# Strassen's scheme for one batch's gate and value products, fewer filler matmuls and operand copies on GpSimd in an attention and gated-layer kernel

## The chip, the cores and the metric

One core of one Trainium2 chip runs the whole program; seven other cores are idle. The metric is the device time of one execution in microseconds (us). Three executions of the kernel before took 910.0, 910.58 and 910.41 us, median 910.41. Engines are called as in the profile: PE (TensorE matmuls), PEld (its weight loads), DVE (VectorE), ACT (ScalarE), POOL (GpSimd), SP (SyncE, which here only issues DMAs).

## The reference

Attention with a pooled query feeds a gated layer; all in float32, with weights that come as 64-bit numbers. The tolerance is that of float32, so the kernel computes most products in split precision (below).

```python
# B, H, S, D = 4, 8, 1152, 64
q_pool = q.reshape(B, H, S // 2, 2, D).mean(axis=3)            # 576 queries a head
scores = np.matmul(q_pool, k.transpose(0, 1, 3, 2)) / np.sqrt(D)
scores = scores - np.max(scores, axis=-1, keepdims=True)
attn = np.exp(scores)
attn = attn / (np.sum(attn, axis=-1, keepdims=True) + 1e-09)
attn_out = np.matmul(attn, v)
x = attn_out.transpose(0, 2, 1, 3).reshape(2304, 512)          # 4 batches of 576 rows
gate = 1.0 / (1.0 + np.exp(-(x @ w_gate)))                     # 512 -> 1536
val = x @ w_val                                                # 512 -> 1536
out = (gate * val) @ w_out                                     # 1536 -> 512
```

## The kernel before

**Split precision.** A float32 operand is stored as two fp32r tiles: a rounded copy `hi` (made by ACT) and the rest `lo` (made by POOL or DVE). A product is three matmuls: hi times hi, hi times lo, lo times hi. Nearly all matmuls stream 288 columns, half of a batch's 576 rows.

**Attention.** 32 heads go in 16 pairs, four pairs to a batch. For each head `head_operands` (L470; `first_head`, L380, for head 0) loads q and k (slots `qr`, `kr`, one each), makes the split operands `QA`/`QB`, `KA`/`KB`, computes the score maxima on PE and DVE (`maxima`, L537, reduction at L550; L452 and L457 for head 0), and writes minus the maximum as a diagonal block into `QB` (`diags`, L371), so that the second score matmul subtracts it. The last 64 queries of both heads of a pair are maximised together from a shared copy `KP`/`QP`, which two DMAs per head (L577, L578) copy from `KA` and `QA`/`QB`. `half` (L624) then does 9 key chunks for each half of the queries: scores (L650), exp (ACT, L654 and L683), its rest (DVE, L686), and the products with v (L693, L697; L668 for the heads of batch 0, `WHOLE`). POOL sums the denominators (L715 to L725), and L770 adds them on PE. `normalise` (L778) divides and splits the result into the `x` tiles.

**Gated layer.** `gated` (L866) runs once a batch: twelve blocks of 128 hidden features in three thirds of four. In each third come four blocks of gate and value (`product`, L877: 4 chunks of the input features by 3 matmuls, 12 matmuls of 288 columns for each block, kind and half: gate to tanh at L929, value times gate at L935, hi at L939, lo at L943) and then four output blocks (`wo`, 12 matmuls for each block and half, added up by L969 and L971). `convert` (L817) turns the 64-bit weights into split float32 during batch 0 and stores them in HBM (`wg_d`, `wo_d`); `weights` (L893) loads them back for each batch. The last batch's wo weights use the three `K` slots, which attention has left by then.

**Warm-up.** `busy` (L989) issues filler matmuls of 192 columns whose result nobody reads, four to a step; `BUSY` (L354) is the number of steps, 18.

**Order.** Each engine runs its instructions in program order, and that order is a table: `Plan.op` lists every step with its engine, and `placed` (L216) puts the steps into the order of `ORDER` and gives each tile the slot that `PLACES` names. The durations, due times and priorities in the calls of `pl.op` are what a planner elsewhere made the tables from; at run time they have no effect. `PSUM` has eight banks (slots `b`).

Of the kernel before, what the change touches and what calls it, by code (L numbers as in the profile page):

```python
# [29 lines left out]
    "YdOSE<z4WC+sJL^UUFNxo$_|h1Dm+T+!oFUOSo-ZB7ng!?hm(*`_1j(zHxiF{agTca(lVI90Ak$yWAHp6*$1{=Du==xn0~3?jU!R`^g>Q4spl0"  # L30
    "@7!$uGB<}m#U1BPb7#1J+zIX+mxiCgr{X#OB$rxD&7bAc^5?lEz~$%iA#d^?AMh8rS^PYH7f*P~TYNe`Gk=Mj$*1S@@fSIp&%*0`0zN;Vhd21F"
    "{7ybEpOBBoXXmr=4xft$d}849G5kF~1CRNPd=5S*pPSz$$LA?X3K%HJCj&+JLVN)}0)_eHARZ{n@8Q#cM0^Us_)MTQA0JfU6Z0kcGJM1r<5Pnx"
    "Tmn#$FU6+?2|*IR5?_KZ36t_=`Qm&Pz8pWFFV9!z7w`x8WPCc11tjNd^4GaSU^!o%uf^BqtMZHal%N`4hhM?h;B$c`{C@rr--ut$rw0xA!~7b4"
    "A-|H}%h%;IfQI}kJ|j5DH|7`dnL!i2IiD3Y<y-P=`F(snzBRv&Z^bv`TkzRH8@@hYUdY5><!*2t_zFThz9Zj>&ki>7TluB@CcZO&pKr^z=W~FY"
# [197 lines left out]
def attention_glu_kernel(ctx: ExitStack, tc: tile.TileContext, qT, kT, vt_in, v, wg, wv, wo, out):  # L232
# [114 lines left out]
    def pool(n, two=True):  # L347
        return 0.18 + 2.35e-3 * n if two else 0.2 + 0.9e-3 * n

    def dma(kb):  # L350
        return 0.15 + kb / 285

    AHEAD = 50
    BUSY = 18  # L354
    KEEP = 0.15
    LAST_GATE = 215
    QLP = lambda u: 1 <= u < 2 * H

    WHOLE = lambda u: u < H
    KLD = lambda u: u >= 16  # L360
# [717 lines left out]
```

## Time and profile before

| | |
|---|---|
| runs | 910.0, 910.58, 910.41 us |
| the profiled execution | 910.93 us |
| its span, first to last instruction | 909.1 us |
| PE busy | 899.6 us (99%), 6371 matmul records |
| DVE, ACT, POOL busy | 651.6, 650.8, 666.7 us |
| moved by DMA | 166.27 MB, 183 GB/s on average |

The profiled execution took 1.8 us more than its span; that is what lies around the instructions. Matmuls are pipelined and the profile models their ends, so two neighbours overlap in "busy"; what one costs is a stretch's time divided by the matmuls that started in it.

### The profile page before, as it was taken

The numbers are of one execution on the slowest core, as the hardware profiler recorded it, in microseconds if no ns is written. First come the engines' busy times: TensorE is split into PE (matmuls) and PEld (weight loads), VectorE is DVE, ScalarE is ACT, GpSimd is POOL, SyncE is SP. The second block draws the span as 40 slices with busy tenths as digits, with TensorE's granted clock in tenths as the row PEclk, the third lists the DMA queues.
The fourth block names the chain that finished last, engine by engine and source line by source line (L and its number), as shares of the span: only waits on it lengthen the run. The fifth ranks groups of instructions, "written<-read, shape, count | busy, mean of one in ns | idle before, by whom it ended". The sixth has DMA issues, their size and how long they took to land.

```text
span 909.1 us, 18593 instructions
## 1 busy us (share of the span) xinstructions
PE 899.6 (99%) x6371; PEld 879.5 (97%) x6371; DVE 651.6 (72%) x1427; ACT 650.8 (72%) x1703; POOL 666.7 (73%) x669
## 2 busy tenths in 40 slices
PE   8999999999999999999999999999999999999998
PEld 7888888999999999999999999999999999999998
DVE  6777788988998998878787887878778774410122
ACT  4878899999998887777777787677787657421211
POOL 6646466989999889988888999888898778521111
PEclk9999999999999999999999999999999999999999
DMA  6898999778887585545563544672734423444532
GB/s 166 226 290 228 279 285 245 241 237 286 294 242 242 175 263 170 158 140 152 154 172 129 137 110 149 209 208 87 195 101 142 152 86 117 143 152 152 186 139 76
DMA packets 57615, 166.27 MB, mean 183 GB/s; under 512 B 17392, under 2 KB 21744, under 8 KB 51376
## 3 DMA queue, kind: packets, MB, share of 16 engines
q1 hardware_dynamic: 57360, 164.78, 60.0%
q8 instruction: 50, 0.82, 0.4%
q14 instruction: 45, 0.37, 0.1%
q10 hardware_dynamic: 160, 0.30, 0.1%
HBM read 132.12 MB, written 23.59 MB: 171 GB/s over the span
## 4 chain that ended last, share of the span: by engine, by line
PE 94%; DVE 3%; DMA 2%; ACT 1%; issue 1%; ACTq 0%; DVEq 0%
PE bank L886 49%; PE bank L650 16%; PE bank L544 8%; PE bank L668 6%; PE bank L693 6%; PE bank L697 6%; PE bank L770 1%; PE bank L991 1%; DMA wg_d<-cs 1%; DMA cr<-in_wv_dram 1%; DVE pm L457 1%; DVE pm L550 1%; ACT e L654 0%; DVE KB L521 0%; DVE el L686 0%
## 5 line engine op out<-in xcount | busy, mean ns | idle before, releaser
L886 PE MATMUL bank<-x,wg 128*128 128x288 f32 x2304 | 371.5, 295 | 0.0
L886 PEld LDWEIGHTS bank<-x,wg 128*128 128x128 f32 x2304 | 331.4, 188 | 0.4
L654 ACT ACTIVATE eh<-bank 128x288 fp32r<-128x288 f32 x432 | 170.9, 411 | 84.0 <-PE bank L650 60.4
L550 DVE TENSOR_REDUCE pm<-bank 128x1 f32<-128x384 f32 x375 | 197.8, 549 | 45.1 <-PE bank L544 41.9
L686 DVE TENSOR_TENSOR el<-bank,eh 128x288 fp32r<-128x288 f32 x432 | 187.5, 451 | 56.1 <-ACT bank L683 26.7
L650 PE MATMUL bank<-QA,KA 128*128 128x288 f32 x576 | 171.0, 303 | 0.4 <-DVE pm L550 0.4
L683 ACT ACTIVATE bank<-bank 128x288 f32<-128x288 f32 x432 | 170.7, 409 | 0.2
L650 PE MATMUL bank<-QB,KB 128*128 128x288 f32 x576 | 166.2, 295 | 1.2 <-DVE QB L375 1.2
L715 POOL TENSOR_TENSOR acc<-acc,eh 128x576 f32<-128x576 f32 x92 | 134.3, 1460 | 18.3 <-ACT eh L654 14.5
L943 POOL TENSOR_TENSOR g<-sg,g 128x288 fp32r<-128x288 f32 x96 | 78.4, 822 | 88.9 <-ACT g L939 86.9
L886 PE MATMUL bank<-g,wo 128*128 128x288 f32 x864 | 143.3, 295 | 0.0
L886 PEld LDWEIGHTS bank<-g,wo 128*128 128x128 f32 x864 | 125.8, 188 | 0.1
L544 PE MATMUL bank<-KA,QA 128*128 128x384 f32 x375 | 121.8, 350 | 0.4 <-DVE pp L550 0.4
L697 PE MATMUL bank<-el,vt 128*128 128x288 f32 x432 | 119.6, 295 | 0.0
L650 PEld LDWEIGHTS bank<-QA,KA 128*128 128x128 f32 x576 | 108.2, 188 | 3.4 <-ACT e L654 0.8
L650 PEld LDWEIGHTS bank<-QB,KB 128*128 128x128 f32 x576 | 108.2, 188 | 2.5 <-issue 1.4
L693 PE MATMUL bank<-eh,vt 128*128 128x288 f32 x432 | 108.5, 295 | 0.0
L935 DVE SCALAR_TENSOR_TENSOR sg<-sg,bank 128x288 f32<-128x288 f32 x96 | 43.0, 449 | 77.5 <-PE bank L886 57.1
L668 PE MATMUL bank<-e,ve 128*128 128x288 f32 x288 | 78.4, 407 | 1.6 <-ACT e L654 1.5
L697 PEld LDWEIGHTS bank<-el,vt 128*128 128x128 f32 x432 | 78.9, 188 | 0.3 <-DVE el L686 0.2
L521 POOL TENSOR_TENSOR KB<-kr,KA 64x576 fp32r<-64x576 f32 x46 | 65.7, 1435 | 17.4 <-ACT KA L515 12.5
L715 POOL TENSOR_TENSOR acc<-eh,eh 128x576 f32<-128x576 f32 x48 | 68.7, 1431 | 10.7 <-ACT eh L654 9.1
(86 smaller groups left out, 1378.1 us busy)
## 6 DMA issues: line engine op xcount, KB each, us to landing
wg<-wg_d SPq DMA_DIRECT2D x48, 1024.0 KB, 5.5
wo<-wo_d SPq DMA_DIRECT2D x36, 512.0 KB, 3.9
kr<-in_kT_dram SPq DMA_DIRECT2D x62, 288.0 KB, 4.9
wg_d<-cs SPq DMA_DIRECT2D x24, 512.0 KB, 5.4
qr<-in_qT_dram SPq DMA_DIRECT2D x31, 288.0 KB, 4.3
KP<-KA SPq DMA_DIRECT2D x30, 288.0 KB, 5.8
vr<-in_v_dram SPq DMA_DIRECT2D x24, 288.0 KB, 4.4
cr<-in_wg_dram SPq DMA_DIRECT2D x12, 512.0 KB, 5.7
```

Source lines behind the costliest of these rows:

```text
L544: nc.tensor.matmul(out=tl(m)[LO if t == 4 else ALL, 0:384], lhsT=lhs(t), rhs=rhs()[:, j * 384:(j + 1) * 384], start=True, stop=True)
L550: nc.vector.tensor_reduce(out=o, in_=tl(m)[p, 0:384], axis=AXX, op=ALU.max)
L650: nc.tensor.matmul(out=tl(m)[:, 0:GN], lhsT=tl(hd["k"])[k][:, ks], rhs=tl(hd["q"])[k][:, a:b], start=(k == 0), stop=(k == 1))
L654: nc.scalar.activation(out=ev(), in_=tl(m)[:, 0:GN], func=ACTF.Exp, scale=1.0 / 16.0)
L668: nc.tensor.matmul(out=tl(av[0])[:, 0:GN], lhsT=pair(c, 0), rhs=tl(h), start=(c == 0), stop=(c == NC - 1))
L683: nc.scalar.activation(out=p, in_=p, func=ACTF.Exp, scale=1.0 / 16.0)
L686: nc.vector.tensor_tensor(out=tl(el), in0=tl(m)[:, 0:GN], in1=ev().bitcast(F32), op=ALU.subtract)
L693: nc.tensor.matmul(out=tl(av[0])[:, 0:GN], lhsT=pair(c, w), rhs=ev(), start=(c == 0), stop=(c == NC - 1))
L697: nc.tensor.matmul(out=tl(av[1])[:, 0:GN], lhsT=pair(c, 1 - w), rhs=tl(el), start=(c == 0), stop=(c == NC - 1 and not mine_c))
L715: nc.gpsimd.tensor_tensor(out=tl(acc), in0=tl(old).bitcast(F32), in1=tl(eh).bitcast(F32), op=ALU.add)
L886: nc.tensor.matmul(out=ps[:, 0:GN], lhsT=l, rhs=r, start=(n == 0 and j == 0), stop=(n == 3 and j == 2))
L943: nc.gpsimd.tensor_tensor(out=g[:, 1, a:b], in0=tl(sg), in1=g[:, 0, a:b].bitcast(F32), op=ALU.subtract)
```

## The change

- The gate and value products of the last batch use Strassen's scheme in Winograd's form: two feature blocks by two halves of the 512 input features by two halves of the rows are seven products of half the depth (2 chunks by 3 matmuls) in place of eight. `gated` calls `two_rows` six times for the last batch, and that calls `seven` once for gate and once for value.
- For this `differences` makes four combinations of the `x` tiles once (T1 to T4: 11 DVE and 4 ACT steps for pair 14, and as many for pair 15), and `combinations` makes four combinations of the weights for each `seven` (S1 to S4: on DVE two additions of 512 columns and four of 256, then two `hi` on ACT and two `lo` of 512 columns on POOL). Products are added up by DVE from the banks.
- The output weights of the last batch lie in the two `wo` slots, no longer in the three `K` slots, which now hold mixed weights (`K`), and each fourth block of gate and value weights lies in `vt0` and `vt1`.
- `BUSY` is 6 in place of 18: 24 filler matmuls in place of 72.
- The `KP`/`QP` copies of pairs 1 to 3 are made by POOL, three copies for each head, in place of DMAs; the other pairs keep the DMAs.
- `FOLD` and `POOLSC` are always false here (u and due are never negative), so their branches do nothing.
- Both tables are new: 7375 steps in place of 7153.

Unpacked, the new `ORDER` says this. **PE** starts with five filler steps (20 matmuls), then the first third of the maxima of query tiles 2, 0 and 1 of head 0, then the sixth filler step, and no filler after it; before, fourteen steps (56) stood ahead of the first maximum and four more among the maxima. **SP** issues v of head 0 (L402) after q and k of head 1; before, it stood ahead of them. **From the last attention matmul (L770) to the last mixing of weights** the table has 528 matmuls on PE; on DVE 19 additions of 512 columns, 40 of 256 and 7 of 288 with both inputs in SBUF, 83 steps of 288 columns with one input in PSUM and one `norm`; on POOL 18 `lo` of 512 columns and 18 steps of 288; on ACT 75 steps. After that 285 matmuls, 46 steps of 288 columns on DVE and 2 and 8 on POOL follow. The last output block weights are loaded when the slot two blocks back is free.

```diff
-    BUSY = 18
+    BUSY = 6
+    KPP = lambda p: p < 4
...
+            if KPP(p):
+                def copy(k, h=h, r=r, w=w):
+                    o, i = (tl(kp)[0][r, SQ * k:SQ * k + SQ], tl(h["k"])[0][r, SQ * k:SQ * k + SQ]) if k < 2 else (
+                        tl(kp)[1][r, 64 * w:64 * w + 64], tl(h["q"])[w][r, 512:SQ])
+                    nc.gpsimd.tensor_copy(out=o, in_=i)
+                for k in range(3):
+                    got.append(pl.op("POOL", 0.7 if k < 2 else 0.2, lambda k=k, copy=copy: copy(k), need - 10 + w, ...
...
+    def differences(p, j, me, nm, s):
...
+            o = pl.op("ACT", act(GN), hi, at, after=after, uses=uses + ([h] if j else []), take=[] if j else [h])
+            x_done["T" + n, j] = pl.op("DVE", dve(GN), lo, at, after=[o], uses=uses + [h])
...
+        o = mix(t1, lambda: b1(0, 1), lambda: b1(0, 0), ALU.subtract, ...
+        o = mix(t1, t1, lambda: b1(1, 1), ALU.add, [old, fh], [o], s - 2)
+        o = mix(t1, t1, lambda: b1(1, 0), ALU.subtract, [old, fh], [o], s - 2)
+        s1 = split("1", t1, [fh], [o], s)
+        t2 = mix(t1, b22, t1, ALU.subtract, [me, fh], [nm, s1], s)
+        split("2", t1, [fh], [t2], s + 0.1)
+        o = mix(b22, b22, lambda: b1(0, 1), ALU.subtract, [me, old], [t2, x_done[p, 1]], s + 0.1)
+        t3 = mix(b22, b22, lambda: b1(1, 1), ALU.subtract, [me, old], [o], s + 0.1)
+        t4 = mix(b21, b21, t1, ALU.subtract, [me, fh], [t2, x_done[p, 0]], s + 0.2)
+        split("3", b22, [me], [t3], s + 0.2)
+        split("4", b21, [me], [t4], s + 0.3)
...
         def weights(kind, m_, at):
-            tag = "K" if kind == "wo" and ch == B - 1 else kind
-            wh = pl.hold(tag)
+            wh = pl.hold(kind)
...
+        def plain(m_, at):
+            whs = [pl.hold("vt0"), pl.hold("vt1")] if m_ % 4 == 3 else [pl.hold("wg")]
...
+        def combinations(i, s):
...
+            fh, sh = pl.hold("kr"), pl.hold("K")
...
+            def full(w, h):
+                nc.vector.tensor_tensor(out=f(h, A), in0=w(0, s, A).bitcast(F32), in1=w(1, s, A).bitcast(F32), op=ALU.add)
...
+            r0 = pl.op("DVE", dve(512), lambda: full(a0, f0), at - 7, after=[l0], uses=w0, take=[fh])
+            r1 = pl.op("DVE", dve(512), lambda: full(a1, f1), at - 7, after=[l1], uses=w1 + [fh])
+            s1 = mix((f1, R), (f1, L), (f1, R), ALU.add, [r1])
+            s3 = mix((f1, L), (f0, L), (f1, L), ALU.subtract, [r0, s1])
+            s2 = mix((f0, L), (f1, R), (f0, L), ALU.subtract, [s1, s3])
+            s4 = mix((f0, R), (f0, R), (f0, L), ALU.subtract, [s2])
...
+                o = pl.op("ACT", act(512), hi, at - 6, after=after, uses=[fh] + ([sh] if k else []), take=[] if k else [sh])
+                done.append(pl.op("POOL", pool(512), lo, at - 6, after=[o], uses=[fh, sh]))
...
+        def seven(i, s, put):
+            sw = combinations(i, s)
...
+                    def mm(j=j, x=x):
+                        for c, (h, l) in enumerate(((0, 0), (0, 1), (1, 0))):
+                            nc.tensor.matmul(out=tl(bank)[:, 0:GN], lhsT=w(h, j), rhs=x(l), ...
...
+            b, p, at = mult("A11", "11")
+            k1 = keep(s1, b, [p], at)
+            b, p, at = mult("S2", "T2")
+            k2 = plus(s2, b, s1, [p, k1], at)
+            b, p, at = mult("A12", "21")
+            put(0, 0, b, s1, [p, k1], at)
+            b, p, at = mult("S1", "T1")
+            k4 = plus(s4, b, s2, [p, k2], at)
+            b, p, at = mult("S3", "T3")
+            u2 = plus(s2, b, s2, [p, k2, k4], at)
+            put(1, 1, b, s4, [p, k4, u2], at)
+            b, p, at = mult("S4", "22")
+            put(0, 1, b, s4, [p, k4], at)
+            b, p, at = mult("A22", "T4")
+            put(1, 0, b, s2, [p, u2], at)
...
+                    nc.vector.tensor_tensor(out=ps, in0=ps, in1=tl(sh), op=ALU.add)
...
+            seven(i, 0, put_gate)
+            seven(i, 1, put_val)
...
+            if ch == B - 1:
+                two_rows(2 * third, gs)
+                two_rows(2 * third + 1, gs)
```

(`keep` is an ACT copy of a bank, `plus` a DVE addition of a bank and a kept tile; `put_gate` adds and takes tanh, `put_val` adds, multiplies by the gate, and splits as L935 to L943 did.)

## Rows read from the trace of the kernel before

**Rows 1.** The page: busy time of engines; the chain that ended last.
```profile
PE 899.6 (99%) x6371; PEld 879.5 (97%) x6371; DVE 651.6 (72%) x1427; ACT 650.8 (72%) x1703; POOL 666.7 (73%) x669
...
PE 94%; DVE 3%; DMA 2%; ACT 1%; issue 1%; ACTq 0%; DVEq 0%
```

**Rows 2.** Stretches: length, busy of PE, PEld, DVE, ACT, POOL (instructions), clock, DMA.
```profile
30.00:60.00 30.00, 30.00 (x164) 26.41 (x162) 23.14 (x48) 26.66 (x64) 16.60 (x16) 1.00 0.98 257
...
150.00:780.00 630.00, 629.25 (x4640) 627.47 (x4639) 514.70 (x1135) 503.86 (x1352) 550.70 (x545) 1.00 0.58 176
...
18.00:790.57 772.57, 770.22 (x5416) 751.26 (x5417) 621.66 (x1353) 622.63 (x1637) 634.90 (x625) 1.00 0.64 190
790.57:906.00 115.43, 115.39 (x870) 115.15 (x869) 20.36 (x48) 22.69 (x57) 20.66 (x26) 1.00 0.39 137
```

**Rows 3.** Busy time by stretch of the filler line L991: length, PE busy (matmuls started).
```profile
2.70:7.90 5.20, 5.17 (x24) 5.17 (x25) 1.00 1.08 249
8.30:11.50 3.20, 3.20 (x31) 3.20 (x30) 1.00 0.87 192
```

**Rows 4.** Timeline of the start: start, length, engine, line, operation.
```profile
6.14 0.55 DVE L418 TENSOR_TENSOR QA<-qr,QA 64x384 fp32r<-64x384 f32 x1
...
11.57 0.71 PE L452 MATMUL bank<-KA,QA 128*128 128x384 f32 x3
...
11.96 4.76 DVE L457 TENSOR_REDUCE pm<-bank 128x1 f32<-128x384 f32 x10 [5.27 <-PE bank L452]
17.89 0.37 PE L650 MATMUL bank<-QB,KB 128*128 128x288 f32 x1 [1.17 <-DVE QB L375]
...
19.85 1.87 PE L668 MATMUL bank<-e,ve 128*128 128x288 f32 x6
```

**Rows 5.** SP's issues at the start; landing of the first v loads (tile ve).
```profile
4.19 0.58 SPq L402 DMA_DIRECT2D ve<-in_v_dram  x1
...
7.96 2.66 SPq L479 DMA_DIRECT2D kr<-in_kT_dram  x2
...
DMA to landing us min/median/max: 4.5/4.6/4.8
```

**Rows 6.** The chain that ended last, 55 to 70 us: start, length, what.
```profile
57.89 7.18 DMA cr<-in_wv_dram
```

**Rows 7.** DVE: groups by shape (busy us, mean ns); two lines' durations (min/median/max ns).
```profile
L686 DVE TENSOR_TENSOR el<-bank,eh 128x288 fp32r<-128x288 f32 x432 | 187.5, 451 | 56.1 <-ACT bank L683 26.7 <-PE bank L697 20.9 <-issue 1.7
L847 DVE TENSOR_TENSOR cs<-bank,cs 128x512 fp32r<-128x512 f32 x36 | 24.3, 681 | 2.4 <-ACT cs L844 2.1
...
L521 DVE TENSOR_TENSOR KB<-kr,KA x16: 754/1183/2465, 315.2 to 723.9; 64x576 fp32r<-64x576 f32 x16
...
L505 DVE TENSOR_TENSOR QA<-qr,QA x16: 752/1150/2012, 307.0 to 702.0; 64x576 fp32r<-64x576 f32 x16
```

**Rows 8.** Timeline of POOL, then of DVE, 380 to 388 us.
```profile
383.40 1.43 POOL L715 TENSOR_TENSOR acc<-acc,eh 128x576 f32<-128x576 f32 x1
...
383.50 1.95 DVE L521 TENSOR_TENSOR KB<-kr,KA 64x576 fp32r<-64x576 f32 x1
...
385.86 0.44 DVE L749 TENSOR_TENSOR y<-bank,t 64x288 f32<-64x288 f32 x1
386.23 0.44 DVE L686 TENSOR_TENSOR el<-bank,eh 128x288 fp32r<-128x288 f32 x1
```

**Rows 9.** POOL groups by shape: busy, mean ns of one.
```profile
L943 POOL TENSOR_TENSOR g<-sg,g 128x288 fp32r<-128x288 f32 x96 | 78.4, 822 | 88.9 <-ACT g L939 86.9 <-issue 1.1 <-ACT sg L929 0.3
L521 POOL TENSOR_TENSOR KB<-kr,KA 64x576 fp32r<-64x576 f32 x46 | 65.7, 1435 | 17.4 <-ACT KA L515 12.5 <-issue 2.5
...
L1033 POOL MEMSET vt<- 128x576 f32 x1 | 0.6, 578 | 0.0
```

**Rows 10.** DMA issues: count, KB each, median us from issue to landing.
```profile
KP<-KA SPq DMA_DIRECT2D x30, 288.0 KB, 5.8
...
KA<-wo_d SPq DMA_DIRECT2D x12, 512.0 KB, 3.7
```

More of the change, by code (lines that the diff above doesn't have):

```diff
@@ L30 @@
[L30 to L34, printed above, removed]
@@ L797, in mult @@
             nc.gpsimd.tensor_tensor(out=y, in0=y, in1=tl(st["r"])[:, a:b], op=ALU.mult)
-        nm = pl.op("DVE", 1.2 if NMP(p) else 1.65, norm, s, after=st["yo"][g], uses=[st["y"], st["r"]], take=[th])
+        nm = pl.op("DVE", 1.2 if NMP(p) else 1.65, norm, s, after=st["yo"][g], uses=[st["y"], st["r"]], take=[tth])
         if NMP(p):
@@ L855, in convert @@
         a0 = pl.op("ACT", act(512), low_bits, due, after=[a], uses=[cr], take=[wd])
-        a = pl.op("ACT", act(512), scale, due, after=[a], uses=[cr])
+        a = pl.op("POOL" if POOLSC(due) else "ACT", act(512), scale, due, after=[a], uses=[cr])
         a = pl.op("DVE", dve(512), sign, due, after=[a, a0], uses=[cr, wd])
@@ new lines, in seven, with mult, plus, add @@
+        def seven(i, s, put):
+            sw = combinations(i, s)
+            s1, s2, s4 = (pl.hold("sg") for _ in range(3))
+            def mult(wname, name):
+                at = now(0.5)
+                wh, w, lw = sw[wname]
+                bank, last = pl.hold("b"), None
+                for j in range(2):
+                    if name in ("11", "21", "22"):
+                        p, hf = 4 * ch + 2 * (name[0] == "2") + j, int(name[1] == "2")
+                        xh, xd = xs[p, 0], x_done[p, hf]
+                        x = lambda l, xh=xh, hf=hf: tl(xh)[:, l, hf * GN:hf * GN + GN]
+                    else:
+                        xh, xd = tb[name[1]], x_done[name, j]
+                        x = lambda l, xh=xh, j=j: t_block(xh, j)[:, l]
+                    def mm(j=j, x=x):
+                        for c, (h, l) in enumerate(((0, 0), (0, 1), (1, 0))):
+                            nc.tensor.matmul(out=tl(bank)[:, 0:GN], lhsT=w(h, j), rhs=x(l),
+                                             start=(j == 0 and c == 0), stop=(j == 1 and c == 2))
+                    last = pl.op("PE", 3 * pe(GN), mm, at + 0.05 * j, after=[last, lw, xd],
+                                 uses=wh + [xh] + ([bank] if j else []), take=[] if j else [bank])
+                return bank, last, at
+            def plus(out, bank, sh, after, at):
+                def add():
+                    nc.vector.tensor_tensor(out=tl(out), in0=tl(bank)[:, 0:GN], in1=tl(sh), op=ALU.add)
+                return pl.op("DVE", dve(GN), add, at - 1, after=after, uses=[bank, sh],
+                             take=[] if out is sh else [out])
+            def keep(out, bank, after, at):
+                def copy():
+                    nc.scalar.activation(out=tl(out), in_=tl(bank)[:, 0:GN], func=ACTF.Copy)
+                return pl.op("ACT", act(GN), copy, at - 1, after=after, uses=[bank], take=[out])
+            b, p, at = mult("A11", "11")
[13 more added lines that the diff above has]
+            put(1, 0, b, s2, [p, u2], at)
@@ L1018, in attention_glu_kernel @@
             pl.op("SP", 0.0, change_pools, PB + 1, after=[o for l in stored.values() for o in l], uses=blocked)
+        for some in later:
+            differences(*some)
         gated(b, PB * (b + 1), PB)
```

476 lines of the change are left out of this document (304 added, 172 removed).

## The prediction

> **What bounds the kernel now.** I first read the page's busy times and the chain that ended last [rows 1]: PE is busy 99% of the span and makes up 94% of the chain, every other engine about 72%. A busy PE is not yet a packed one, so next come the stretches [rows 2]. From 18 us to the last attention matmul PE has 2.35 us without work in 772.57. In the 115.43 us that follow it starts 870 matmuls, one per 0.1327 us, with 0.04 us idle, while DVE works 20.36 us, ACT 22.69 and POOL 20.66. So in this tail a matmul less is 0.1327 us less, for as long as DVE, ACT and POOL stay out of the way. The third view is the start [rows 3, 4]: PE runs fillers from 2.73 us and the first real matmul starts at 11.57, although the DVE step that it needs (L418) ended at 6.69. The fillers go at 0.217 us each (5.20 us by 24) before 7.9 us and at 0.103 (3.20 by 31) after 8.3: the lower and the upper level of the clock (1.2 and 2.4 GHz), which the clock column does not tell apart here. The last views are of the engines that get the new work: what DVE and POOL pay for such shapes, and what they do to each other [rows 7 to 9].
>
> The sum is made against the profiled execution, 910.93 us, 0.5 above the median of the runs; about 0.2%, 1.8 us, is what a measurement of this kernel can tell from no change.
>
> **Fewer matmuls.** Twelve rounds (six block pairs by gate and value) of 7 products by 6 matmuls are 504, where 12 by 2 by 2 by 12 were 576. 72 by 0.1327 us [rows 2] is **9.55 us less**, all of it on the path if PE stays packed.
>
> **Fewer fillers.** The 16 fillers among the maxima filled time in which PE waited for DVE, so removing them gives nothing. Ahead of the first maximum 20 are left: 2.73 + 20 by 0.217 is 7.1 us in place of 11.57, 4.5 earlier, and its operands are there at 6.69 [rows 4]. After it DVE sets the pace (ten reductions in 4.76 us), so the shift carries on to the first complete scores (17.89, then 13.4) and to the first product with v (19.85, then 15.4). That product needs v of head 0, now issued behind q and k of head 1, whose issue ends at 10.62 [rows 5]; 0.58 of issue and 4.6 of landing give at most 15.8. I take **4.3 us less**, between 0 and 4.5.
>
> **The rest of batch 0.** Everything then comes 4.3 us earlier into a stretch where ACT works 26.66 of 30 us and DMA is 98% busy [rows 2]. The KP copies leave SP's queue and the DMA engines: 6 heads by 304 KB, some 7 us at 257 GB/s, and a landing of 5.8 us each [rows 10]. POOL gets 12 copies of 64x576 and 6 small ones. No row shows a copy on POOL; the nearest are a MEMSET of 576 columns (0.578) and a two-input step (1.435) [rows 9], so 7 to 17 us plus about 2. With one input I take the low end. Behind the copies in POOL's queue stand the next heads' rests and diagonals, and PE's scores wait for those; POOL's idle time covers it (16.60 of 30 us busy from 30 to 60), so it costs nothing; without that cover up to 1.4 us a head. PE's largest wait so far lay behind a weight load of 7.18 us in ACT's queue [rows 6]; it may go with the lighter DMA. Bounds: 2.35 us gained (all of PE's idle time up to the tail) to 3 lost (ACT's 26.66 of 30 leave 3.34 free). I take **0.5 us more**.
>
> **DVE in the tail.** Back to back, a DVE step of 288 columns costs 0.37 us (385.86 to 386.23) [rows 8], 0.08 less than its duration of 0.45; likewise 512 columns 0.60 (0.681), and 256 columns, read between the two, 0.34 [rows 7]. From the last attention matmul to the last mixing of weights DVE has 19 by 0.60, 40 by 0.34, 90 by 0.37 and about 1.0 for the norm: 59.3 us. PE has 528 by 0.1327: 70.1. Undisturbed, DVE keeps up, and nothing is lost.
>
> But 66 of these steps read both inputs from SBUF, and such steps are disturbed by POOL. L521 on DVE takes 0.754 us at best and 1.183 in the median, L505 0.752 and 1.150 [rows 7]: 0.41 more. At 383.50 one took 1.95 us [rows 8]; POOL had begun a step of 1.43 us just before it, and DVE's step ended about half a microsecond after POOL's: it stood still meanwhile. The median loss belongs to a stretch in which POOL is busy 87% (550.70 of 630) [rows 2]. In the tail POOL has 18 steps of 512 columns (1.30, read between 0.822 and 1.435 [rows 9]) and 18 of 0.82: 38.2 of 70.1 us, 54%. I scale 0.41 by 54 over 87: 0.25 us a step, 16.8 in all, so DVE needs 76.1 us and is 6 behind PE. PE can run ahead by the banks it still has free; I allow three products of six matmuls, 2.4 us. The lag peaks inside the stretch, not at its end, so I take **4 us more**. Bounds: 0, and 13.9 at the unscaled 0.41 (66 by 0.41 is 27.1; 59.3 + 27.1 - 70.1 - 2.4).
>
> The Trainium skill states this as a rule (GPSIMD Engine Reference, Specifications): GpSimd's SBUF interfaces are shared with VectorE, and contention is with VectorE steps in a two-port mode or with two SBUF inputs. By that rule the 66 steps pay and the 83 others do not; the trace agrees: L686, with one input in the banks, stays at 0.451 in the mean of 432 [rows 7].
>
> **The rest of the tail.** POOL's 38.2 us and ACT's 75 steps, at the tail's 0.40 (22.69 by 57 [rows 2]) 30 us, lie beside PE's 70.1 and stay hidden. The differences T of the last pair make the last-attention chain longer (on DVE behind POOL's multiplication, then ACT, then DVE: three steps of about 0.45); products of the plain tiles and the rest of batch 2's layer cover that, and without them it would cost 1.4. The gate and value loads are as many bytes as before, covered as before. The output weights have two slots in place of three: a block's 24 matmuls take 3.2 us, a load 3.7 [rows 10], so in the last third, where nothing is left to fill, a block waits 0.5, with the issue 0.7. The last round's additions have no next round behind them: 0.3. Together **1.0 us more**, between 0 and 2.5.
>
> **Sum.** 910.93 - 9.55 - 4.3 + 0.5 + 4 + 1.0 = 902.6 for a profiled execution, less 0.5: **902.0 us**.
>
> **Rivals.**
> - *The tail stays packed* (chance 0.27). POOL and DVE fall between each other, the lag fits the banks: 902.0 - 4 = 898.0. For it speaks that DVE has 11 us to spare undisturbed; against it the medians of rows 7.
> - *The start gives nothing* (0.13): 902.0 + 4.3 = 906.3. With 20 fillers PE begins the maxima before 8 us, then waits for DVE (three matmuls in 0.71 us [rows 4], where DVE takes 0.476 for each); if the clock falls back to 1.2 GHz there, 4.3 us of PE work take twice as long. Against it: before, PE waited 1.17 us for the diagonal [rows 4] and the scores behind it still came at the upper level.
> - *VectorE becomes the bound and the kernel is slower* (0.10). Place: the rounds in the tail. Each of the 66 steps finds POOL at work, as in attention, because the mixing of one round meets the rests of the last. Price 0.41 us a step: 13.9 us against the other terms' 12.35, 910.4 - 12.35 + 13.9 = 912.0. It decides from 0.39 us a step on.
>   The skill's rule, taken strictly (a two-input step waits whenever GpSimd is at work), is this rival.
> - *The new order leaves gaps elsewhere* (0.05). From 150 to 780 us PE misses 0.75 us [rows 2]; the new table need not be as tight. At 5 us more: 907.0.
> - *The change does not do what it says*: two of its switches are never on, but products, fillers and copies change in the code itself; I give it no chance of its own.
>
> **How the numbers follow.** The forecast holds 0.45. The range reaches from 895.5 (no loss in the tail, and part of PE's idle time gone) to 909.0 (the start's gain lost, and some of DVE's bound with it); about 0.15 is outside, most of it above. Faster than 908.6: the forecast, the packed tail, the lost start and part of the others, 0.87; within 0.2% 0.05; slower 0.08, from VectorE as the bound and a bad order.
>
> **What would show it.** PE has 120 matmuls fewer. The first maximum starts near 7.1 us and the first complete scores near 13.4, with matmuls of 288 columns 0.13 us apart from there on; if they are 0.25 apart, the clock has fallen. In the tail DVE is busy over 75% in place of 18%, additions of 512 columns with two SBUF inputs take 0.68 us alone and over a microsecond beside POOL, and PE's waits name DVE steps, some 4 us of them in the first two thirds. If PE's gaps there are below 1 us, the packed tail was right; above 12 us, VectorE is the bound. The forecast would be wrong in its reason if the tail lost time to loads or to ACT.

## The result: slower by 1.1%, where faster by 0.9% was forecast

The changed kernel took 918.85, 919.11 and 921.15 us, median 919.11; the kernel before beside it takes 910.2 in the median of four. The ratio of the means is 1.0109, 95% interval 1.0084 to 1.0133. A fourth execution of the changed kernel ran in a slow state, 1239.58 us at a granted clock of 0.655, and is left out (with it the median is 920.13). The profiled execution is the one of 919.11 us, its span is 917.3.

The page of the changed kernel, busy time and the chain that ended last (as [rows 1]):

```profile
PE 894.9 (98%) x6251; PEld 869.0 (95%) x6251; DVE 749.6 (82%) x1605; ACT 671.2 (73%) x1747; POOL 714.1 (78%) x711
...
PE 83%; DVE 9%; DMA 3%; issue 2%; POOL 1%; ACT 1%; SPq 0%; DVEq 0%; ACTq 0%; POOLq 0%
```

The 120 matmuls are gone. But DVE is 9% of the chain in place of 3, and its busy time grew by 98 us for 178 more instructions, 0.55 us each, where 0.34 to 0.60 were forecast for one back to back and undisturbed, and 0.25 more for one with two SBUF inputs. The stretches from 740 us on (columns as in [rows 2]):

```profile
740.00:752.00 12.00, 7.45 (x39) 6.69 (x38) 11.55 (x17) 2.44 (x7) 7.14 (x9) 0.74 0.00 0
752.00:806.00 54.00, 50.32 (x364) 48.62 (x364) 47.37 (x87) 33.37 (x93) 41.53 (x38) 0.99 0.34 115
806.00:860.00 54.00, 50.88 (x372) 49.31 (x371) 50.61 (x105) 22.08 (x53) 27.57 (x25) 1.00 0.54 184
860.00:913.80 53.80, 52.32 (x385) 50.95 (x383) 33.85 (x77) 13.30 (x32) 18.54 (x20) 1.00 0.33 113
```

In the first stretch PE starts 39 matmuls in 12 us, at a granted clock of 0.74. From 806 to 860 DVE is busy 94% of the time, and 372 matmuls start where 407 would fit at 0.1327 us. What happens at 743 is in the timelines of POOL and DVE and in the view of PE's waits:

```profile
742.89 0.80 POOL L746 TENSOR_TENSOR acc<-acc,eh 128x288 f32<-128x288 f32 x1
743.65 0.80 POOL L846 TENSOR_TENSOR x<-y,x 128x288 fp32r<-128x288 f32 x1
744.40 0.80 POOL L1209 TENSOR_TENSOR g<-sg,g 128x288 fp32r<-128x288 f32 x1
745.15 2.29 POOL L846 TENSOR_TENSOR x<-y,x 128x288 fp32r<-128x288 f32 x3
...
742.48 0.54 DVE L559 TENSOR_REDUCE pm<-bank 128x1 f32<-128x384 f32 x1
742.95 4.81 DVE L875 TENSOR_TENSOR QA<-vr,QA 128x288 fp32r<-128x288 f32 x1
747.68 1.01 DVE L559 TENSOR_REDUCE pm<-bank 128x1 f32<-128x384 f32 x2
...
PE bank L553 <- DVE pm L559: 3.8, 1, 3.8
```

L875 is the rest of T1 of pair 14: both inputs in SBUF, 288 columns, 0.45 us when alone. It began 0.06 us after the start of a POOL step and ended 0.3 us behind the end of the last of six POOL steps that followed each other without a pause. Behind it in DVE's queue stood the maxima of the last head, and PE's next matmul in order waited for them: no matmul starts from 744.2 to 748.3. The fifteen of 288 columns after that start 0.24 us apart, from 752.7 on 0.133: PE came back at the lower level of its clock (1.2 GHz), which cost another 15 by 0.107 = 1.6 us.

To see where time went over the whole run I added up PE's **loss**: for each pair of neighbouring matmuls the distance of their starts beyond the undisturbed one (0.1327 us for 288 columns, 0.176 for 384, 0.111 for a filler, 0.2425 for L689, L668 before). By stretch, in us:

| kernel | 0–30 | 30–160 | 160–740 | from 740 |
|---|---|---|---|---|
| before | 5.0 | 3.2 | 0.7 | -0.2 |
| changed | 7.9 | 1.3 | 1.7 | 20.7 |

The balance of the two profiled executions: 72 matmuls less are -9.55, 48 fillers less -5.3 (48 by 0.111), the losses +2.9, -1.9, +1.0 and +20.8, behind the last matmul +0.15: together +8.1, and 919.11 - 910.93 is 8.18. Of the +1.0 between 160 and 740 us, 1.1 is one wait for output weights at 289 us, which the traces of no other run in this order show.

Of the 20.7 us, 12.7 are lost ahead of the last attention matmul (L794, at 797.8 us) and 8.0 behind it. Ahead of it, 7.1 us fall up to 752 us, the stall above. Most of the rest are five waits of 0.5 to 1.1 us (4.5 together) for `el` (L707), the exp's rest of the last attention heads. Those steps stand in DVE's queue behind the first sums and mixes of the weights (L1028, L1031) and T steps of pair 15 (L875), and these run beside POOL's last denominators (L736, L743, L746) and first rests (L1048). One of the five, from the timelines of POOL, DVE and PE:

```profile
771.74 3.05 POOL L736 TENSOR_TENSOR acc<-acc,eh 128x576 f32<-128x576 f32 x2 [0.36 <-ACT eh L675]
...
771.97 3.11 DVE L1031 TENSOR_TENSOR kr<-kr 128x256 f32<-128x256 f32 x2
775.00 0.45 DVE L707 TENSOR_TENSOR el<-bank,eh 128x288 fp32r<-128x288 f32 x1
...
775.50 0.40 PE L714 MATMUL bank<-eh,vt 128*128 128x288 f32 x1 [0.81 <-DVE el L707]
```

### The profile page after: what moved, and what is told of

Same layout as the page of the kernel before. It is cut to its first block, busy times and chain, and to the rows that moved or that the text cites. A ratio compares the mean times of both kernels' runs of the same rounds, so it can differ in the third digit from the quotient of the medians.

```text
span 917.3 us, 18691 instructions
## 1 busy us (share of the span) xinstructions
PE 894.9 (98%) x6251; PEld 869.0 (95%) x6251; DVE 749.6 (82%) x1605; ACT 671.2 (73%) x1747; POOL 714.1 (78%) x711
## 4 chain that ended last, share of the span: by engine, by line
PE 83%; DVE 9%; DMA 3%; issue 2%; POOL 1%; ACT 1%; SPq 0%; DVEq 0%; ACTq 0%; POOLq 0%
PE bank L970 37%; PE bank L671 16%; PE bank L553 8%; PE bank L689 7%; PE bank L718 6%; PE bank L714 6%; PE bank L1082 2%; DVE kr L1031 2%; DVE kr L1028 1%; DMA wo<-wo_d 1%; PE bank L794 1%; DVE bank L1128 1%; DMA vt<-wg_d 1%; DVE sg L1092 1%; DVE el L707 1%
## 5 line engine op out<-in xcount | busy, mean ns | idle before, releaser
L970 PE MATMUL bank<-x,wg 128*128 128x288 f32 x1728 | 289.5, 296 | 0.5 <-DVE pm L559 0.5
L970 PEld LDWEIGHTS bank<-x,wg 128*128 128x128 f32 x1728 | 254.2, 188 | 0.8 <-DVE pm L559 0.7
L707 DVE TENSOR_TENSOR el<-bank,eh 128x288 fp32r<-128x288 f32 x432 | 187.5, 451 | 45.1 <-ACT bank L704 24.1
L970 PE MATMUL bank<-g,wo 128*128 128x288 f32 x1152 | 188.1, 296 | 3.1 <-DMA wo<-wo_d 1.2
L970 PEld LDWEIGHTS bank<-g,wo 128*128 128x128 f32 x1152 | 165.6, 188 | 5.7 <-ACT t L1141 1.3
L736 POOL TENSOR_TENSOR acc<-acc,eh 128x576 f32<-128x576 f32 x92 | 134.5, 1462 | 16.1 <-ACT eh L675 12.4
L553 PE MATMUL bank<-KA,QA 128*128 128x384 f32 x375 | 125.0, 353 | 4.3 <-DVE pm L559 4.1
L718 PE MATMUL bank<-el,vt 128*128 128x288 f32 x432 | 117.3, 295 | 0.9 <-DVE el L707 0.9
L714 PEld LDWEIGHTS bank<-eh,vt 128*128 128x128 f32 x432 | 76.4, 188 | 2.1 <-DVE el L707 1.0
L689 PE MATMUL bank<-e,ve 128*128 128x288 f32 x288 | 77.9, 406 | 0.0
L530 POOL TENSOR_TENSOR KB<-kr,KA 64x576 fp32r<-64x576 f32 x46 | 67.6, 1475 | 12.0 <-ACT KA L524 5.8
L553 PEld LDWEIGHTS bank<-KA,QA 128*128 128x128 f32 x375 | 68.8, 188 | 7.1 <-DVE pm L559 4.7
L736 POOL TENSOR_TENSOR acc<-eh,eh 128x576 f32<-128x576 f32 x48 | 68.8, 1433 | 8.4 <-ACT eh L675 7.0
```

Source lines behind the costliest of these rows:

```text
L530: e.tensor_tensor(out=tl(kh)[1][HI, s], in0=tl(kr)[HI, s], in1=tl(kh)[0][HI, s].bitcast(F32), op=ALU.subtract)
L553: nc.tensor.matmul(out=tl(m)[LO if t == 4 else ALL, 0:384], lhsT=lhs(t), rhs=rhs()[:, j * 384:(j + 1) * 384], start=True, stop=True)
L689: nc.tensor.matmul(out=tl(av[0])[:, 0:GN], lhsT=pair(c, 0), rhs=tl(h), start=(c == 0), stop=(c == NC - 1))
L707: nc.vector.tensor_tensor(out=tl(el), in0=tl(m)[:, 0:GN], in1=ev().bitcast(F32), op=ALU.subtract)
L714: nc.tensor.matmul(out=tl(av[0])[:, 0:GN], lhsT=pair(c, w), rhs=ev(), start=(c == 0), stop=(c == NC - 1))
L718: nc.tensor.matmul(out=tl(av[1])[:, 0:GN], lhsT=pair(c, 1 - w), rhs=tl(el), start=(c == 0), stop=(c == NC - 1 and not mine_c))
```

## The experiments

Theory one at the outset: DVE steps with both inputs in SBUF stand still while POOL works, for longer than the forecast allowed, and at 743 us such a stall reaches PE and its clock. Rivals: the amount of new work on DVE, the new order, the start, the copies on POOL. Ratios are to the kernel before on the same chip.

**1. Only the stalled step on POOL.**

```diff
+    TLO = {("1", 0)}
...
-                nc.vector.tensor_tensor(out=t[:, 1], in0=src(), in1=t[:, 0].bitcast(F32), op=ALU.subtract)
+                e = nc.gpsimd if (n, j) in TLO else nc.vector
+                e.tensor_tensor(out=t[:, 1], in0=src(), in1=t[:, 0].bitcast(F32), op=ALU.subtract)
```

> The changed kernel with one step moved: the rest of T1 of pair 14 (L875, 288 columns, both inputs in SBUF) goes from DVE to POOL. On DVE it took 4.81 us while POOL ran steps back to back, PE stood still for 4.0 us behind it and then ran at 1.2 GHz until 752.7 us; PE's lost time from 740 to 753 us is about 7 us. Theory one (a DVE step with two SBUF inputs stands still for as long as POOL has the next step ready): the stall and the slow clock go, 919 becomes 912 to 914. Rival (DVE has too much to do there, whatever POOL does): the wait moves to the next DVE step, and less than 2 us come back.

915.51 us, ratio 1.0064 (1.005 to 1.0078), 4.6 us back. The clock stayed at 1.0, but the next DVE step with two SBUF inputs inherited the stall (its timeline):

```profile
746.39 4.21 DVE L885 TENSOR_TENSOR vr<-x 128x288 f32<-128x288 f32 x1
```

PE found work beside it and stood still only 2.0 us. What follows: the stall belongs to this place in the order, not to L875 alone.

**2. The rests of the mixed weights and of gate times value by ACT.**

```diff
-                    nc.gpsimd.tensor_tensor(out=t[:, 512:1024], in0=f(h, A), in1=t[:, 0:512].bitcast(F32), op=ALU.subtract)
+                    nc.scalar.activation(out=t[:, 512:1024], in_=f(h, A), func=ACTF.Copy)
...
-                    nc.gpsimd.tensor_tensor(out=tl(g)[:, 1, a:b], in0=factor(r, hf), in1=tl(g)[:, 0, a:b].bitcast(F32),
-                                            op=ALU.subtract)
+                    nc.scalar.activation(out=tl(g)[:, 1, a:b], in_=factor(r, hf), func=ACTF.Copy)
```

> The changed kernel with the rests of the mixed weights and of gate times value of the last batch taken off POOL: ACT makes them as plain copies. Left out: the subtraction, so these rests hold the number and not its remainder. DVE's work is the same. Theory one: without POOL steps in the tail the two-input DVE steps run at their undisturbed 0.45 to 0.68 us, and most of PE's 8.5 us of lost time after the last attention matmul goes; the 7 us stall before it, where POOL works for attention, stays: 911 to 914. Rival (amount of DVE work): PE's lost time after the last attention matmul stays above 5 us, and the time above 915.

914.17 us, ratio 1.0057 (1.0036 to 1.0078). From the last denominator (L794) to the last matmul it takes 110.5 us (798.69 to 909.18) in place of 115.9 (797.77 to 913.70); the 813 matmuls there are 107.9 by 0.1327. So of 8.0 us lost behind attention 5.4 are POOL's doing, and 2.6 stay. The stall (4.80 us) and the low clock stayed, as they should.

**3. The changed kernel with 72 fillers** (`range(4)` to `range(12)` in each of the six steps).

> The changed kernel with 72 fillers again, 12 in each of its six steps: 60 stand ahead of the first maximum and 12 behind the third. If the fillers cost the start what stands ahead of the first maximum, the first maximum moves from about 7 us to 11.5 to 12 and the time grows by 4 us, to 923. Rival (the start waits for DVE and for loads anyway, and without fillers the clock rises later): less than 1.5 us more, or none.

921.95 us, ratio 1.0134 (1.012 to 1.0148), against 1.0109 for the changed kernel: the fewer fillers are worth some 2.3 us here, between the two expectations. In the two traces they are worth more at the start: from the 60th to the 300th matmul behind the fillers this kernel is 4.1 us later than the changed one, and 2.8 from 322 us on, where the changed one has had its wait of 1.1 us at 289.

**4. The kernel before with 24 fillers.**

```diff
-        def busy():
-            for _ in range(4):
+        def busy(k):
+            for _ in range(4 if k < 5 or k == 14 else 0):
...
```

> The kernel before with one part of the change alone: 24 fillers, 20 ahead of the first maximum and four behind the third. As forecast for this part: 4.3 us less, 906. From the changed kernel, whose PE gained about 2.4 us up to 30 us: 2 to 3 us less, 907.5 to 908.5. Rival (the first scores wait for operands that were hidden behind the fillers, or the clock falls): within 1 us of 910.

906.41 us, ratio 0.9966 (0.9955 to 0.9976): 3.3 us faster than the kernel before, and the fastest version with the whole computation in this study. In the two traces it is 3.9 us ahead from the 60th to the 150th matmul behind the fillers. So this part of the change is good and the rest loses 13. Its start beside the changed kernel's, from the two timelines, first the kernel before with 24 fillers:

```profile
6.16 0.55 DVE L418 TENSOR_TENSOR QA<-qr,QA 64x384 fp32r<-64x384 f32 x1
...
7.11 1.22 PE L452 MATMUL bank<-KA,QA 128*128 128x384 f32 x3
```

then the changed kernel:

```profile
6.16 1.40 POOL L441 TENSOR_TENSOR KB<-kr,KA 64x576 fp32r<-64x576 f32 x1 [0.68 <-DMA qr<-in_qT_dram]
...
6.46 1.51 DVE L427 TENSOR_TENSOR QA<-qr,QA 64x384 fp32r<-64x384 f32 x1 [0.44 <-ACT QA L422]
...
8.03 1.33 PE L461 MATMUL bank<-KA,QA 128*128 128x384 f32 x3 [0.72 <-DVE QA L427]
...
16.79 1.64 PE L689 MATMUL bank<-e,ve 128*128 128x288 f32 x6
```

The new order puts POOL's rest of k (L441) in front of DVE's rest of q, which then takes 1.51 us in place of 0.55: the same effect in small. It makes the first maximum 0.9 us later, and the first product with v comes at 16.79 us, where this kernel has it at 15.90.

**5. and 9. The disputed cost by itself**, in two small kernels. A trial in the second (`two` is a subtraction of two inputs, `step` the DVE step that is measured):

```diff
+        for k, p in enumerate(outs):
+            if copies:
+                nc.gpsimd.tensor_copy(out=p[:, 0:288], in_=c[:, 0:288])
+            else:
+                two(nc.gpsimd, p, c, b, 288)
...
+        two(nc.vector, dw, bank, a, 288)
+        step(do[name])
```

> This kernel computes nothing of the reference: it only measures the disputed cost. Each trial starts VectorE and GpSimd together; VectorE does one step with a PSUM operand (0.45 us) and then the step measured, GpSimd a chain of n subtractions of two SBUF operands (288 columns, 0.75 us apart) that wait for nothing. Theory one (a VectorE step with two SBUF operands gets through only when GpSimd has no step ready, so it waits for the whole chain): the measured step takes about 0.45 us alone, up to 0.8 beside a chain of 1, about 1.5 beside 2, 3 beside 4, 4.3 beside 6, about 3.7 beside 3 steps of 576 columns; of four steps behind each other beside a chain of 6 the first takes the 4.3 and the others 0.45 each; with a PSUM operand each of four takes 0.45 beside the same chain; beside copies of one operand the step is nearer to 0.45. Rival (it waits for no more than the GpSimd step under way): at most 0.45 + 0.8 = 1.25 us whatever the length of the chain, and four steps beside a chain of 6 take some 0.8 to 1.25 each.

> As the first measuring kernel (nothing of the reference is computed), but each step of a GpSimd chain writes a tile of its own. In the first one all steps of a chain wrote one tile, so each waited for the one before it and began some 80 ns behind its end, and VectorE's step took 0.84 us beside chains of any length; in the changed kernel the steps beside the long VectorE steps begin some 45 ns ahead of the end of the one before. Theory (VectorE's two-operand step gets in only where GpSimd pauses between two steps; steps that wait for nothing leave no pause): chains of 1, 2, 4, 6 and 8 free steps make VectorE's step 0.8, 1.6, 3.1, 4.6 and 6.1 us; of three steps the first takes 4.6 and the others 0.45 each; a copy of one column that waits for the step before it, put behind the second and fourth step, brings it to about 1.6, behind every step to 0.84; the chain on one tile gives 0.84 again; with a PSUM operand 0.45. Rival (the length of the chain has nothing to do with it, what stalled VectorE in the kernel is a wait that the trace does not show): 0.84 beside every chain.

DVE's groups in the first (busy us, mean ns; `chain` are chains of 1, 2, 4 and 6 steps, `wide` of steps of 576 columns, `four` and `psum` four steps beside a chain of 6, `copies` POOL copies with one input):

```profile
L39 DVE TENSOR_TENSOR four<-a,d 128x288 f32<-128x288 f32 x12 | 10.9, 908 | 0.3
L39 DVE TENSOR_TENSOR chain<-a,d 128x288 f32<-128x288 f32 x12 | 10.0, 836 | 0.0
L39 DVE TENSOR_TENSOR psum<-bank,a 128x288 f32<-128x288 f32 x12 | 5.5, 455 | 0.3
L39 DVE TENSOR_TENSOR wide<-a,d 128x288 f32<-128x288 f32 x3 | 4.3, 1446 | 0.0
...
L39 DVE TENSOR_TENSOR copies<-a,d 128x288 f32<-128x288 f32 x3 | 1.4, 459 | 0.0
L39 DVE TENSOR_TENSOR alone<-a,d 128x288 f32<-128x288 f32 x3 | 1.3, 449 | 0.0
```

and in the second, with a tile of its own for each POOL step (`free`: chains of 1 to 8, min/median/max ns):

```profile
L41 DVE TENSOR_TENSOR free<-a,d x15: 773/777/780, 18.7 to 152.6; 128x288 f32<-128x288 f32 x15
```

Both times the rival won: DVE gets in when the POOL step under way ends, whatever the length of the chain; pauses in the chain changed nothing here (0.84 and 0.77 us). With one input in PSUM DVE loses nothing. The trial with POOL copies settles nothing: DVE's step began 0.15 us before the first copy's end, so at most that was at stake, and the second copy took 0.54 and 0.66 us in place of 0.43 and 0.42. So the common loss is what is left of one POOL step, 0.3 to 1.0 us, and my theory of the whole chain is not the rule. In the changed kernel's trace it is the exception too. Of 134 DVE steps with both inputs in SBUF 49 have no POOL step beside them, 17 end before the POOL step beside them, 65 behind the first POOL step that ends, and 3 behind a later one, among them the L875 of 4.81 us. But in 43 of the 65 POOL had paused by then or had nothing more to do; in 22 its next step had begun, and DVE got in all the same.

**6. The steps behind T1 on POOL too** (`(p, j) == (14, 0)`: eight steps of `split` and `mix`).

> The changed kernel with all sums and rests that pair 14 makes for the last batch's gated layer behind its own output (eight steps of 288 columns) on GpSimd in place of VectorE, so that VectorE has no step with two SBUF operands between 743 and 751 us; the sums of old blocks ahead of them and pair 15's steps stay on VectorE. Theory one (the 4.8 us step, the 4 us gap of TensorE and the slow clock behind it cost some 7 us; in the kernel with only the first rest moved the next such step inherited half): neither stall is left, granted clock 1.0 from 740 to 752, 919.1 - 7 = 911 to 913 us. Rival (the stall goes to the next VectorE step with two SBUF operands wherever it stands, or GpSimd's later steps come too late): 915 to 919, with a TensorE gap of over 1.5 us between 740 and 765 again.

914.89 us, ratio 1.0047 (1.003 to 1.0064), at the edge of the rival's range. The rival was right that the stall goes on wandering, now to a sum of pair 15's (DVE's timeline, and the last POOL step beside it):

```profile
744.96 5.71 DVE L886 TENSOR_TENSOR vr<-x 128x288 f32<-128x288 f32 x1
...
749.56 0.79 POOL L1213 TENSOR_TENSOR g<-sg,g 128x288 fp32r<-128x288 f32 x1
```

Here eight POOL steps follow each other, each starting some 40 ns ahead of the end of the one before, and DVE ends 0.3 us behind the last.

**7. The rests on DVE** (`nc.gpsimd` to `nc.vector` in both places of experiment 2).

> The changed kernel with the 24 rests of the mixed weights (512 columns) and the 24 rests of gate times value (288 columns) on VectorE in place of GpSimd: GpSimd has almost nothing left behind the attention's end. VectorE gets 24 x 0.68 + 24 x 0.43 = 26.5 us more of undisturbed work and loses the waits of its 48 mixes (0.588 mean against 0.42) and 24 sums (0.96 against 0.68), some 15 us. Theory one (the tail loses time because steps wait for GpSimd, not because VectorE has too much work): 8 us lost behind the attention's end become 3 to 5, 914 to 917 us. Rival (VectorE's amount of work binds there): 919 or more, with VectorE over 90% busy behind the attention's end.

922.3 us, ratio 1.0136 (1.0114 to 1.0157): the rival. The mixes got cheaper (0.520 us in place of 0.588, additions 0.757 in place of 0.973), but from 799.7 to 917 us DVE is busy 101.3 of 117.3 us, 86% and not over 90, and in the profiled execution (925.62 us) 13.8 us are lost behind attention in place of 8.0. In this order DVE can't take the rests as well.

**8. The copies of pairs 1 to 3 by DMA again**, where the third of POOL's copies stood.

> The changed kernel with the shared operands of pairs 1 to 3 copied by DMAs again, as in the kernel before, and not on GpSimd; all else and the order stay. Theory one (the copies on GpSimd took two waits of TensorE for a DMA out of batch 0, some 2.7 us): 2 to 3.5 us slower than the changed kernel, TensorE's loss between 30 and 160 us up from 0.9 to about 3.5. Rival (the forecast: the copies are worth nothing or cost up to 0.6 us each, and the new order took the waits out): within 0.7 us of the changed kernel.

939.71 us, ratio 1.0319 (1.0291 to 1.0347). PE's waits:

```profile
PE bank L553 <- DMA KP<-KA: 9.3, 1, 9.3
PE bank L553 <- DMA kr<-in_kT_dram: 7.1, 1, 7.1
```

Twenty us more is neither theory. One wait is for a copy itself, the other for a load of k that SP issues behind the copies (78.78 us, the copies at 75.41 and 78.09). So the run tells about the DMAs' place in this order and nothing about what the copies on POOL are worth. Experiment 13 asks again.

**10. and 11. A pause between POOL's steps** from 727 us on, and the mixed weights' rests also cut in two.

```diff
+    def pool_step(out, **kw):
+        nc.gpsimd.tensor_tensor(out=out, **kw)
+        if cutting[0]:
+            nc.gpsimd.tensor_copy(out=cut_to, in_=out[:, 0:1].bitcast(F32))
```

> The changed kernel with a GpSimd copy of one column, which waits for the step before it, behind most GpSimd steps from 727 us on (products and rests of the attention's output, last sum of a denominator, rests of gate times value and of the mixed weights; 71 copies, some 0.2 us each). No other work moves, VectorE keeps all its steps. Theory (a pause between GpSimd's steps lets VectorE in): the 4.8 us step becomes at most 1.2 us, no TensorE gap of over 1.5 us between 740 and 752, clock 1.0 there, and some of the losses further on go too: 909 to 912.5 us. Rival (the stall has another cause, or moves on as it did in the two kernels that moved steps to GpSimd): 915 to 920.

> As the kernel with the one-column copies, and the 24 rests of the mixed weights (512 columns, 1.3 us each) as two steps of 256 columns with a pause between them. Theory (a VectorE step waits for what GpSimd has under way, so shorter GpSimd steps cost it less): the sums of 512 columns fall from a mean of 0.96 to about 0.85 us and the total is 1 to 2.5 us below the kernel with the copies alone. Rival (what is lost behind the attention's end is GpSimd's time itself, the rests that TensorE waits for): equal or slower by up to 2 us.

915.54 us, ratio 1.0062 (1.0046 to 1.0079), and 918.01, ratio 1.0091 (1.0076 to 1.0106). In the first, the T1 rest and the stretch of the stall:

```profile
742.39 1.05 DVE L882 TENSOR_TENSOR QA<-vr,QA 128x288 fp32r<-128x288 f32 x1
...
740.00:752.00 12.00, 11.27 (x78) 10.34 (x77) 11.75 (x25) 7.40 (x22) 11.26 (x19) 1.00 0.19 60
```

No step was moved, only pauses were added: 4.81 us became 1.05, 39 matmuls became 78, the clock 1.00. So breaking the chain of POOL steps ends the stall at this place, and the stall with the clock behind it is worth 5 us (loss from 740 to 760: 7.25 before, 2.2 now). The total stayed above the 909 to 912.5 that I expected: POOL is busy 17 us more from 740 us on (111.8 against 94.8), and the loss behind 760 us rose from 13.4 to 15.3. Cutting steps in two made it worse by 2.5 us, more than its rival allowed, though the sums of 512 columns did fall, from 0.835 to 0.740 us in the mean: there POOL's own time counts.

**12. All rests of the tail by ACT.** (In `pool_step` of experiment 10, an ACT copy in place of the subtraction.)

> The changed kernel in which, from 727 us on, every rest that GpSimd makes of the attention's output, of gate times value (both kinds) and of the mixed weights is an ACT copy of the same size (leaves out these subtractions; GpSimd keeps the denominators' sums and the products with the inverses, VectorE keeps all its steps). The upper bound of what GpSimd's part costs in the tail. Theory one (GpSimd's steps, by holding VectorE and by what waits for them, cost most of the 20.7 us that TensorE lost between 740 and 914): at most 7 lost there, 904 to 908 us. Rival (the new chain of sums, mixes and additions on VectorE costs most of it, whatever GpSimd does): 12 or more lost, 911 us or more.

905.51 us, ratio 0.9954 (0.9936 to 0.9972). The page's stretches and DVE's groups:

```profile
740.00:752.00 12.00, 11.21 (x77) 10.20 (x77) 10.60 (x25) 8.89 (x27) 4.82 (x6) 1.00 0.19 68
752.00:806.00 54.00, 51.55 (x380) 50.10 (x378) 45.79 (x99) 37.01 (x101) 24.70 (x23) 1.00 0.42 147
806.00:860.00 54.00, 54.00 (x407) 53.82 (x406) 47.43 (x111) 37.63 (x93) 0.00 (x0) 1.00 0.50 173
```

```profile
L1036 DVE TENSOR_TENSOR kr<-wg 128x512 f32<-128x512 f32 x18 | 13.1, 737 | 0.4 <-ACT KB L299 0.3
L1039 DVE TENSOR_TENSOR kr<-kr 128x256 f32<-128x256 f32 x48 | 24.6, 513 | 0.9
```

and in the changed kernel

```profile
L1028 DVE TENSOR_TENSOR kr<-wg 128x512 f32<-128x512 f32 x18 | 17.3, 973 | 0.8 <-POOL KB L1048 0.8
L1031 DVE TENSOR_TENSOR kr<-kr 128x256 f32<-128x256 f32 x48 | 28.2, 588 | 0.9
```

The time is theory one's. With DVE's steps and the order untouched, 407 matmuls start from 806 to 860 us, as many as fit. The loss from 740 on is 7.6 us in place of 20.7: POOL's rests cost 13 of them. Of the 7.6, 5.9 lie ahead of the last attention matmul (790.2 us), where POOL still makes denominators (busy 24.70 of 54 us from 752 to 806), and 1.7 behind it. So behind attention DVE's new work costs little once POOL is out of the way; how much of the 5.9 is DVE's work alone, no run separates.

**13. The copies on POOL in the old order**, on top of experiment 4.

```diff
+                if p < 4:
+                    for a in (0, SQ):
+                        nc.gpsimd.tensor_copy(out=tl(kp)[0][r, a:a + SQ], in_=tl(h["k"])[0][r, a:a + SQ])
+                    nc.gpsimd.tensor_copy(out=tl(kp)[1][r, 64 * w:64 * w + 64], in_=tl(h["q"])[w][r, 512:SQ])
+                    return
```

> The kernel before with 24 fillers, and the shared operands of pairs 1 to 3 copied by GpSimd, three copies where the two DMAs of a head were issued; order and plain last batch stay. Theory one (the copies take two waits of TensorE for DMAs out of batch 0, some 2.5 us): 903 to 905 us, TensorE's loss between 30 and 160 us 1.5 or less. Rival (the forecast's: hidden, or 0.6 us a copy on the way): 906 to 908 us.

907.02 us, ratio 0.9964 (0.995 to 0.9979); experiment 4 had 0.9966: the copies are worth nothing, the rival. PE's losses in the runs that this rests on, in us:

| kernel | 0–30 | 30–160 | 160–740 | from 740 |
|---|---|---|---|---|
| 4: before, 24 fillers | 6.4 | 1.3 | 0.9 | -0.1 |
| 3: changed, 72 fillers | 6.7 | 1.2 | 0.5 | 20.5 |
| 1: T1 rest on POOL | 8.1 | 1.5 | 1.5 | 16.9 |
| 2: last layer's rests by ACT | 10.4 | 1.5 | 0.7 | 14.6 |
| 10: pauses | 8.3 | 1.6 | 0.5 | 17.5 |
| 12: tail's rests by ACT | 8.0 | 1.3 | 1.0 | 7.6 |
| 13: 4 and copies on POOL | 7.5 | 0.9 | 2.1 | -0.2 |

## Why the prediction was wrong

**Fewer matmuls: right.** PE's work fell by the 9.55 us, and in experiment 12 they went through at 0.1327 us each for 54 us on end. The change does what it says.

**Fewer fillers: right; the new order at the start was left out.** 4.3 us forecast. With the order unchanged, the traces give 4.1 (experiment 3) and 3.9 (experiment 4) at the start; of the runs' times 2.3 and 3.3 are left. But by 30 us the changed kernel has gained only 2.4 (48 fillers, 5.3, less 2.9 lost): its new order loses 7.9 us there and the old one with 24 fillers 6.4. The first maximum came at 8.03 and not at 7.1, the first product with v at 16.79 and not at 15.4 to 15.8. What held it was not the load of v but, for 0.9 us, DVE's rest of q beside POOL's rest of k. I had read that operand as there at 6.69 from the old order [rows 4] and not asked what the new one puts beside it.

**The rest of batch 0: wrong sign, inside its bounds.** +0.5 forecast, -1.9 measured. The copies cost POOL 0.66 us each, the low end that I took, and are hidden, as costed (experiment 13). The gain is mostly one wait of 1.6 us at 64.5 us in the trace of the kernel before, behind the weight load of [rows 6]. It is gone with 24 fillers in the old order (1.3 lost, experiment 4) and with 72 in the new one (1.2, experiment 3); so either change is enough, and what removes it stays open.

**DVE in the tail: the step that failed.** +4 forecast behind the last attention matmul, at most 13.9, and 1.0 for the rest of the tail with the T blocks hidden; measured 8.0 behind that matmul and 12.7 ahead of it.
- *The place.* I counted only steps behind the last attention matmul. The costliest one stood ahead of it, at 743 us, among the T blocks of pair 14. I had priced those of pair 15 alone, three steps of 0.45, under "the rest of the tail", and taken them as hidden. At 743 DVE's queue holds the last head's maxima, and no bank is ahead: 4.0 us of PE, and 1.6 at the lower clock. Behind it the first mixes and pair 15's T steps hold up attention's exp rests (4.5 us in five waits). The row that would have warned me was L521's 2.465 us [rows 7], longer than any one POOL step; I used the median.
- *The price.* "0.25 us a step", scaled from the medians of [rows 7] by how busy POOL is, took a stall for a share of a POOL step. The small kernels give 0.33 to 0.46 a step of 288 columns whenever POOL is at work, 1.0 beside a POOL step of 576: nearer to the unscaled 0.41 of the rival. Additions of 512 columns lost 0.23 to 0.29 against the 0.68 that they take with POOL out of the way.
- *What was right in it.* "Undisturbed, DVE keeps up, and nothing is lost" holds behind the last attention matmul to within 1.7 us (experiment 12), and from 806 to 860 us all 407 matmuls go through. What the sum of work does not show is where a step stands in DVE's queue: from 752 to 806 us, where attention's last steps wait behind the mixes, 380 of 407 start in that run.

**The rest of the tail.** Its items (1.0 us) can't be told from the above; waits for the output weights were 0.4 us in experiment 12. The T blocks that I took as hidden under this heading are in the 12.7 us above.

**The rivals.** "VectorE becomes the bound", 0.10, was right in kind and its 912.0 still 7 short: it knew the price, but neither the stall at 743 nor the rests that PE's products wait for. The Trainium skill (SBUF — State Buffer, Summary: rules for kernel authors) says that of a VectorE step with two SBUF inputs and a GpSimd step that reads SBUF the second to start is blocked until the first has finished. The small kernels agree (0.84 and 1.45 us); L875's 4.81 us, six POOL steps long, goes beyond it. The other rivals are out: the tail was not packed, the start gave 2.4 us, and of PE's waits from 740 us on 0.3 us name loads and 1.3 ACT.

Of the 17.1 us between 902.0 (the terms as rounded give 902.1) and 919.1, POOL's rests in the tail account for 13.1 (experiment 12) and the tail's other losses beyond the 5 forecast for 2.6. The start adds 1.9 (2.4 gained, where 4.3 were forecast), the stretch from 160 to 740 us 1.0, and 0.5 comes of the profiled execution (at the median here, 0.5 above it before); batch 0 gave 2.4 back. That makes 16.7.

**Open:** why DVE got in at the first end of a POOL step in the small kernels and in 65 cases of the changed kernel, but at 743 us not for six. In the 22 cases where POOL's next step had already begun, that step was held up in its turn (0.97 to 1.33 us in place of 0.80 for one of 288 columns); at 743 us each of the six took no longer than 0.80. A pause ends it (experiment 10), moving the step does not (1 and 6); a length of the chain alone does not cause it (9).

## What to carry to other kernels

Work taken off the bound engine was paid for by two engines that get in each other's way: before giving DVE steps with both inputs in SBUF to a stretch, look at what POOL does in it, step by step, and at what stands behind them in DVE's queue; a step with one input in PSUM lost nothing (0.455 us beside a chain of POOL steps). Use the longest row of a group and not its median where one late step stops the bound engine, and count every stretch in which new steps stand, also the one ahead of the stretch that they serve. Here the small part alone (24 fillers, 906.41 us) is the version to keep: even with POOL's rests in the tail gone, the seven products only draw level with it (905.51; ratios 0.9954 and 0.9966).

## What was not expected of the hardware

A DVE step of 0.45 us took 4.81, 4.21 and 5.71 us beside 6 to 8 POOL steps without a pause, in three kernels, and 1.05 with a pause between them. It is no accident of one execution: L875 takes 4.80 to 4.82 us in experiments 2, 3, 7 and 8 too, which leave the steps around it as they are (in 8 it stands at 761 us). The kernel before has a smaller one, L521 at 633 us, 2.17 us through the ends of three POOL steps, and in experiment 13 the same step takes 3.34 us through four. Behind a gap of 4.0 us PE's matmuls started 0.24 us apart for 4.4 us (granted clock 0.50 from 748 to 751), behind one of 3.1 us (experiment 6) for 3.0 (0.51 from 751 to 754); behind one of 2.0 us (experiment 1) only two single ones did, and the granted clock stayed at 1.00. And six pairs of DMAs, put where POOL's copies had stood, cost 20 us (experiment 8).
